# Attention times values with the exponentials standing and 65 value columns passing, division per token, and x turned by the DMA crossbar

## Chip, cores and metric

One core of one Trainium2 chip. The metric is the device time of one execution in microseconds (us), median of several runs. TensorE (PE) has a granted clock that the profile reports beside each stretch; on one core a run cannot be compared with a second die, so a run counts as fast when it lies within 1.5% of the fastest of its kernel.

## The reference

Eight batches of eight heads, 576 tokens, head dimension 64, with a bias that depends on the distance of two tokens and is constant beyond 128; then a feed-forward layer that takes the elementwise maximum of three products.

```python
scores = scale * np.matmul(q, k.transpose(0, 1, 3, 2)) + bias
attn = np.exp(scores - max);  attn = attn / (attn.sum(-1) + 1e-09)
x = (attn @ v).transpose(0, 2, 1, 3).reshape(B * S, H * D)      # 4608 x 512
h = np.maximum(np.maximum(x @ w1, x @ w2), x @ w3)              # d_ff = 768
return h @ w_out                                               # 4608 x 512
```

## The kernel before

Keys lie on the partitions: a score tile holds 128 keys by queries, for two heads (a "head pair") at once. Each head pair of each batch is visited in two halves of 256 queries. The 64 tokens beyond 512 are handled apart: "left keys" (tile `et`) and "left queries" (`scq`). The exponential is multiplied by the exponential of the bias in the band near the diagonal. Attention times values, called the attend, keeps values and a block of 64 ones columns in the array and lets 288 query columns pass. The result comes out with head dimensions on partitions (the form that the FFN wants), and 64 rows of it repeat the row sum.

```python
def attend(b, hp, e4, et, lo, hi, pool=ps_a):       # ps_a: one pair of banks
    ...
    for par in range(2):                             # left keys
        mm(x[par][:, 0:n], lhsT=vt[b % 2][r, hp, :], rhs=et[r, lo:hi], start=True, stop=False)
    for par in range(2):
        for t in range(KT):                          # 4 key tiles, 288 columns each
            mm(x[par][:, 0:n], lhsT=vx[b % 2][:, t, v0 : v0 + P], rhs=e4[:, t, par, lo:hi], ...)
    for par in range(2):                             # reciprocal as exp(-ln(sum)), on ScalarE
        nc.scalar.activation(out=ld[r, 0:n], in_=x[par][d, 0:n], func=ACTF.Ln)
    nc.scalar.activation(out=rd[:, 0:n], in_=ld[:, 0:n], func=ACTF.Exp, scale=-1.0)
    def quotients():                                 # VectorE
        for par in range(2):
            nc.vector.tensor_tensor(out=xT[hp][r, ...], in0=x[par][r, 0:n], in1=rd[r, 0:n], op=ALU.mult)
```

Between the attention instructions the loop puts pieces of the FFN of the batch before. Each product of 512 columns takes one bank of PSUM, the memory that TensorE writes its results to, from a pool of two (`ps_f`); ScalarE copies the first (`m`), VectorE takes the maximum with the second (`m`) and with the third (`hT`), and then the bank is free. The output product goes through `osb` to memory. All stores of `osb` and, from batch 2 on, all q and k transposes are issued by Sync, in program order; before the change the ten transposes for the next batch stand in one block at its first head pair.

```python
    visit(qT, kT, e4, 1)                             # scores and exponentials, second half
    quotients = next_late()                          # emits the attend of a pair before
    times_band(hp, e4, 1, 0, QM)                     # band products on VectorE
    times_band(hp, e4, 2, 0, QM)
    ...
    fill(rate, quotients, lambda: left_queries(qT, kT, e4))     # FFN pieces, quotients among them
```

The softmax here doesn't subtract the row's maximum and nothing guards it: scores larger than these inputs give would overflow.

## Time and profile before

| | before |
|---|---|
| median | 367.65 us (367.58 to 368.91, 3 runs) |
| TensorE, ScalarE, VectorE busy | 335.9, 273.9, 241.8 us |
| batch 1 begins / batch 2's second head pair begins | 45.4 / 94.9 us |
| from there to the end of the span of 367.5 | 272.6 us |
| one half in the middle of the kernel (first, second) | 4.62, 4.57 us |

The starts in the table are those of the first score matmul of a visit in TensorE's timeline. I use 94.9 us as the border of two regions: before it no engine is full, behind it TensorE is. Three of the groups with shapes kept apart (columns: line, engine, operation, result and operand with shapes, count; busy us and mean ns of one; idle time before them and its releaser) belong to the work that the change removes:

```profile
L477 DVE TENSOR_TENSOR xT<-a,rd 64x288 bf16<-64x288 f32 x112 | 50.9, 455 | 28.9 <-ACT rd L472 27.0
L471 ACT ACTIVATE ld<-a 64x288 f32<-64x288 f32 x112 | 45.4, 405 | 10.0 <-PE a L92 7.3
L472 ACT ACTIVATE rd<-ld 128x288 f32<-128x288 f32 x56 | 24.7, 442 | 1.6
```

VectorE waited 27 us for ScalarE's `rd`, but VectorE is not the bound, so this idle time alone costs nothing. What counts is how often TensorE waited for the same chain, and TensorE's waits (total us, times, longest) say: not much.

```profile
PE a L92 <- DVE xT L477: 3.8, 9, 0.9
PE sc L92 <- ACT et L407: 3.4, 5, 0.8
```

### The profile page before, as it was taken

To read this page: it belongs to the slowest core of one execution; us is meant where nothing else is said; L and a number is where in the kernel's file an instruction comes from. 1 tells how busy PE (TensorE), PEld (TensorE's weight loads), DVE (VectorE), ACT (ScalarE), POOL (GpSimd) and SP (SyncE) were. 2 spreads that over 40 slices of the span, in tenths; PEclk is the share of its full clock that TensorE was granted. 3 is DMA by queue.
4 is the path that set the end of the run, shared out by engine and by line. 5 is a ranking of instruction groups with operands and counts; after the bars stand their busy time and mean duration, and the time that the engine had idled before them with its cause. 6 is when DMAs were issued, how large, how long until landed. Compare 5 with 4: busy or idle time off the path is not lost.

```text
span 367.5 us, 6415 instructions
## 1 busy us (share of the span) xinstructions
PE 335.9 (91%) x2364; PEld 185.6 (51%) x2396; DVE 241.8 (66%) x505; ACT 273.9 (75%) x456; POOL 114.4 (31%) x150
## 2 busy tenths in 40 slices
PE   2777888888999999999999999999999999999995
PEld 1444665555455555555555555555555455444442
DVE  6685766555477766776777677777777677545352
ACT  4996897777699988997899889988998798222221
POOL 8736764993850055405550500050000000000000
PEclk9998999988899999999999999999999999999999
DMA  9999999999991099909990992099201100110303
GB/s 163 210 210 160 159 148 144 186 104 142 126 186 12 2 142 150 160 2 119 156 179 3 112 136 75 2 93 142 88 3 57 59 0 2 71 46 0 114 0 117
DMA packets 154600, 36.56 MB, mean 99 GB/s; under 512 B 146624, under 2 KB 149960, under 8 KB 154568
## 3 DMA queue, kind: packets, MB, share of 16 engines
q0 software_dynamic: 109568, 16.59, 65.4%
q1 hardware_dynamic: 43944, 19.29, 25.1%
q8 instruction: 19, 0.31, 0.3%
q10 hardware_dynamic: 1056, 0.26, 0.3%
q14 instruction: 13, 0.11, 0.1%
HBM read 35.39 MB, written 9.45 MB: 122 GB/s over the span
## 4 chain that ended last, share of the span: by engine, by line
PE 72%; ACT 15%; DVE 6%; issue 4%; DMA 1%; another core or an unknown queue 1%; SPq 0%; DVEq 0%; ACTq 0%
PE ps L92 34%; PE a L92 17%; PE pso L92 8%; PE sc L92 8%; ACT e L407 8%; ACT ld L471 3%; PE scq L92 2%; DVE xT L477 2%; DVE osb L313 1%; ACT rd L472 1%; PE sct L92 1%; ACT et L407 1%; DVE hT L300 1%; DMA xT<-in_q_dram 1%
## 5 line engine op out<-in xcount | busy, mean ns | idle before, releaser
L92 PE MATMUL ps<-xT,w_bf 128*128 128x512 bf16 (+1 forms) x695 | 153.2, 360 | 5.2 <-DVE osb L313 2.2
L407 ACT ACTIVATE e<-sc 128x1024 bf16<-128x1024 f32 x128 | 124.1, 1021 | 28.5 <-PE sc L92 28.3
L92 PEld LDWEIGHTS <-w_bf 128*128 128x128 bf16 x720 | 69.1, 99 | 60.5 <-issue 5.0
L401 DVE TENSOR_TENSOR e<-e,band 128x768 bf16<-128x768 bf16 (+4 forms) x140 | 65.2, 477 | 29.5 <-ACT e L407 25.8
L477 DVE TENSOR_TENSOR xT<-a,rd 64x288 bf16<-64x288 f32 (+2 forms) x128 | 58.2, 455 | 32.0 <-ACT rd L472 29.8
L92 PE MATMUL a<-e,vx 128*128 128x288 bf16 (+2 forms) x512 | 76.2, 292 | 0.6 <-DVE e L401 0.6
L92 PEld LDWEIGHTS <-kT 64*128 64x128 bf16 (+1 forms) x740 | 40.8, 97 | 50.5 <-issue 30.5
L92 PEld LDWEIGHTS <-vx 128*128 128x128 bf16 x512 | 45.5, 99 | 29.5 <-issue 18.1
L471 ACT ACTIVATE ld<-a 64x288 f32<-64x288 f32 (+2 forms) x128 | 51.8, 405 | 10.4 <-PE a L92 7.3
L276 ACT ACTIVATE m<-ps 128x512 bf16<-128x512 f32 x54 | 31.7, 587 | 34.0 <-PE ps L92 31.8
L92 PE MATMUL pso<-wo_bf,hT 128*128 128x512 bf16 x209 | 50.7, 380 | 1.3 <-DVE hT L300 0.5
L295 DVE TENSOR_TENSOR m<-ps,m 128x512 bf16<-128x512 f32 x54 | 37.4, 692 | 20.7 <-ACT m L276 15.6
L92 PE MATMUL sc<-qT,kT 64*128 64x256 bf16 x512 | 42.2, 281 | 6.8 <-ACT et L407 3.4
L300 DVE TENSOR_TENSOR hT<-ps,m 128x512 bf16<-128x512 f32 x54 | 37.2, 689 | 15.0 <-PE ps L92 13.7
L155 POOL DMA_DIRECT2D vt<-in_v_dram x16 | 10.2, 655 | 83.6 <-PE a L92 83.6
L147 POOL DMA_DIRECT2D q_sb<-in_q_dram x28 | 25.0, 909 | 31.3 <-DMA qT<-q_sb 27.0
L92 PEld LDWEIGHTS <-hT 128*128 128x128 bf16 x216 | 20.4, 98 | 22.2 <-DVE hT L300 2.1
L472 ACT ACTIVATE rd<-ld 128x288 f32<-128x288 f32 (+2 forms) x64 | 28.3, 441 | 1.7
L147 POOL DMA_DIRECT2D vx<-in_v_dram x32 | 28.5, 928 | 0.2 <-issue 0.2
L147 POOL DMA_DIRECT2D k_sb<-in_k_dram x28 | 24.8, 919 | 11.8 <-DMA w_bf<-in_moe_w_dram 6.8
L313 DVE COPY osb<-pso 128x512 f32<-128x512 f32 x32 | 21.9, 685 | 6.1 <-PE pso L92 5.6
L92 PE MATMUL a<-et,vt 64*128 64x288 bf16 (+2 forms) x128 | 22.3, 286 | 3.8 <-DVE xT L477 3.8
(53 smaller groups left out, 158.8 us busy)
## 6 DMA issues: line engine op xcount, KB each, us to landing
out_dram<-osb SPq DMA_DIRECT2D x36, 256.0 KB, 2.4
vx<-in_v_dram POOLq DMA_DIRECT2D x32, 128.0 KB, 6.0
q_sb<-in_q_dram POOLq DMA_DIRECT2D x28, 128.0 KB, 5.4
k_sb<-in_k_dram POOLq DMA_DIRECT2D x28, 128.0 KB, 5.6
w_bf<-in_moe_w_dram POOLq DMA_DIRECT2D x3, 768.0 KB, 13.5
xT<-in_k_dram SPq DMA_DIRECT2D x6, 128.0 KB, 4.1
wo_bf<-in_moe_w_out_dram POOLq DMA_DIRECT2D x1, 768.0 KB, 7.7
qtail<-in_q_dram POOLq DMA_DIRECT2D x16, 32.0 KB, 5.6
```

What stands on the lines that cost most here:

```text
L92: inorder(nc.tensor.matmul(*args, **kw))
L147: nc.gpsimd.dma_start(out=dst[:, t, h0:h1, :], in_=x[:, t, h0:h1, :])
L155: nc.gpsimd.dma_start(out=diag(dst[b % 2], par, h0, h1), in_=tail_part(src, b, h0, h1, par))
L276: nc.scalar.activation(out=st[fb]["m0"][:], in_=st[fb]["ps0"], func=ACTF.Copy)
L295: nc.vector.tensor_tensor(out=m[:], in0=st[fb]["ps1"], in1=st[fb]["m0"][:], op=ALU.max)
L300: nc.vector.tensor_tensor(out=hT[:, fb * CH : fb * CH + CH], in0=ps2, in1=st[fb]["m"][:], op=ALU.max)
L313: nc.vector.tensor_copy(osb[:], ps[:])
L401: nc.vector.tensor_tensor(out=e4[:, t, :, lo:hi], in0=e4[:, t, :, lo:hi], in1=band[hp][:, :, lo - P * t + P : hi - P * t + P], op=ALU.mult,)
L407: nc.scalar.activation(out=out_, in_=in_, func=ACTF.Exp, scale=inv_sqrt_d)
L471: nc.scalar.activation(out=ld[r, 0:n], in_=x[par][d, 0:n], func=ACTF.Ln)
L472: nc.scalar.activation(out=rd[:, 0:n], in_=ld[:, 0:n], func=ACTF.Exp, scale=-1.0)
L477: nc.vector.tensor_tensor(out=xT[hp][r, b * S + lo : b * S + hi], in0=x[par][r, 0:n], in1=rd[r, 0:n], op=ALU.mult,)
```

## The change

The intent is to swap the operands. The exponentials (128 keys by 128 queries) stand in the array and 65 value columns pass, 64 dimensions and one column of ones. The result then has one token per partition with its sum beside it; the quotient needs one reciprocal per token and head, on VectorE, and the Ln and Exp on ScalarE disappear. In return x is the wrong way round for the FFN, so five crossbar transposes (DMA transfers that transpose on the way, here issued by Sync) per batch turn it (batch 0 is turned on TensorE). The attend's PSUM is now one bank, used in turn with a second. The q and k transposes are spread over three head pairs in place of one block. The diff also puts more FFN pieces into each half of batch 1 (a `rate` of 8 in place of 1) and starts each FFN chunk a half or more later.

```diff
-    ps_a = ctx.enter_context(tc.tile_pool(name="ps_a", bufs=1, ...))      # two tags: one pair of banks
+    ps_a = ctx.enter_context(tc.tile_pool(name="ps_a", bufs=2, ...))      # one tag: two banks in turn
...
-                    x[par][:, 0:n], lhsT=vx[b % 2][:, t, v0 : v0 + P],
-                    rhs=e4[:, t, par, lo:hi], start=False, stop=(t == KT - 1),
...
-            nc.scalar.activation(out=ld[r, 0:n], in_=x[par][d, 0:n], func=ACTF.Ln)
-        nc.scalar.activation(out=rd[:, 0:n], in_=ld[:, 0:n], func=ACTF.Exp, scale=-1.0)
...
+                x[:, 2 * i : 2 * i + 2, :], lhsT=et[:, c], rhs=vl[:, hp, :, 0:AW],          # 130 columns
...
+                        x[:, 2 * i + par, :], lhsT=e4[:, kt, par, c], rhs=v[:, kt, 2 * hp + par, 0:AW],   # 65
...
+            nc.vector.reciprocal(rd[:, 0:n], x[:, 0:n, D])
+            nc.vector.tensor_tensor(out=x_sb[b][...], in0=x[:, 0:4, 0:D]..., in1=rd[:, 0:4]..., op=ALU.mult)
...
+            if b and hp == HP - 1:
+                for t in range(2 * half, 2 * half + 2 + half):
...
+                    inorder(nc.sync.dma_start_transpose(out=xT[:, :, c : c + w], in_=x_sb[b][0:w, t, :]))
...
-                nxt = transposes(b + 1)
...
+        if hp in (1, 2) and b + 1 < B:
+            next(crossbar)                            # two of the ten, five times per batch
```

## The prediction

> **What bounds the kernel now.** I read the page's busy shares first, then the waits of TensorE, then the chain of waits over one batch in the middle, and last the groups of instructions with shapes kept apart. The span is 367.5 us. Busy shares from part 1 of the page:
>
> ```profile
> PE 335.9 (91%) x2364; PEld 185.6 (51%) x2396; DVE 241.8 (66%) x505; ACT 273.9 (75%) x456; POOL 114.4 (31%) x150
> ```
>
> A busy PE proves little, because matmul ends are modelled. The table of 20 us stretches separates two regimes (columns: stretch, PE, PEld, DVE, ACT and POOL busy us with counts, clock, DMA share, GB/s):
>
> ```profile
> 40.00:60.00 20.00, 16.82 (x162) 11.40 (x163) 13.40 (x31) 17.64 (x29) 10.19 (x14) 1.00 1.99 154
> 60.00:80.00 20.00, 16.39 (x157) 11.34 (x155) 12.71 (x28) 15.84 (x27) 19.10 (x25) 1.00 1.84 147
> ...
> 220.00:240.00 20.00, 19.90 (x142) 10.69 (x144) 14.28 (x27) 18.30 (x32) 0.00 (x0) 1.00 0.12 40
> ```
>
> Until about 95 us no engine is full and ACT is the busiest. After that PE is full. The chain of waits in that later region (start, us, what) shows the order of one visit:
>
> ```profile
> 185.13 0.54 PE sc L92 x8
> 185.67 1.21 PE a L92 x10
> 186.88 0.05 issue
> 186.93 1.67 PE ps L92 x7
> 188.61 0.22 PE scq L92 x4
> 188.83 0.87 PE ps L92 x4
> 189.70 0.54 PE sc L92 x8
> ```
>
> Every link is PE: one visit (half a head pair) is 4.57 us, of which the attend "a" is 1.21 us. Once per batch the chain leaves PE (208.1 to 212.5 us: exp, ld, ld, rd, xT, osb), some 0.7 us more than PE work there. A batch repeats every 37.6 us (first score matmuls at 161.2, 198.8 and 236.4 us in the timeline). So the later region pays by PE stream time alone.
>
> The early region is different. In the timeline at 66 to 72 us PE stands 0.67 us for "ACT et", then 0.86 and 0.21 us for "DVE xT". The exponential of the left keys waits behind two Ln, which wait for the attend; the next attend waits until the quotients have freed its single pair of banks.
>
> **What the Trainium skill says.** "TensorE: Matmul & The Clock Gate", section "Back-to-back issue gap", gives N / 2.4 + 2.5 ns warm for an isolated matmul, and about 81 ns per LDWEIGHTS and MATMUL pair at N = 128 as the sustained figure. The same page, "LDWEIGHTS (loading the stationary operand)", gives columns / 1.2, so 107 ns for 128 columns. If either slow figure held, the change would lose. The trace disagrees with both:
>
> ```profile
> 201.35 0.44 PE L92 MATMUL sct<-qT,kT 128*128 128x512 bf16 x3
> 203.77 1.15 PE L92 MATMUL a<-e,vx 128*128 128x288 bf16 x8
> 206.06 0.39 PE L92 MATMUL scq<-qT,kT 128*128 128x128 bf16 x4
> ...
> L92 PE MATMUL sct<-qT,kT 128*128 128x64 bf16 x64 | 7.1, 193 | 0.0
> L92 PEld LDWEIGHTS <-vx 128*128 128x128 bf16 x512 | 45.5, 99 | 29.5 <-issue 18.1 <-DMA q_sb<-in_q_dram 0.4
> ```
>
> The first row is one 512-column and two 64-column matmuls, each with its own 128-column load. It ends 0.44 us after its start; less the last one's 193 ns, the third starts 0.25 us in. The 512 columns take 0.216 (1/2.4 ns each plus 2.5), so the two 64-column ones start about 30 ns apart (28 in the single records). The 288-column ones go at (1.15 - 0.29)/7 = 123 ns, the 128-column ones at (0.39 - 0.22)/3 = 57 ns. A load is shown as 99 ns, but is pipelined ahead and costs the stream nothing. Columns count, not loads.
>
> "VectorE: DVE Perf Modes", section "The TRN2 errata — SBUF-src ops pay a fixed extra latency per instruction", has (N + 151)/0.96 ns for an fp32 tensor_tensor; for 288 elements that is 457, and the quotient rows show 455. I use it for DVE.
>
> "DMA: Bandwidth & Descriptors", section "DMA Transpose (X-bar)", says the plain transpose is issued from Sync or Scalar only and takes 2-byte data. Here all 60 are on SP:
>
> ```profile
> 204.98 5.35 SPq L360 DMA_TRANSPOSE qT<-q_sb  x4
> ```
>
> so about 1.3 us of issue each, and the page's part 6 counts 4 to 5.4 us to landing.
>
> **The change part by part.** *Attend on PE.* Before, one attend is two tail matmuls that run side by side (64-row halves) and eight of 288 columns: 120 + 95 (the load exposed where 64-row tiling ends) + 8 x 123 = 1.20 us. After, the exponentials stand and 65 columns pass: the first half is 2 matmuls of 130 columns (57 ns) and 16 of 65 (65/2.4 + 2 = 29.5 ns), 0.586 us, plus the same 95 ns of exposed load, 0.68 us. The second half adds 5 of 130 columns, 0.97 us. A head pair goes from 2.40 to 1.65 us: 0.75 us saved, although matmuls rise from 20 to 41. The left keys keep their time (512+128 columns for 512+64+64). From 95 us to the end there are 48 of the 64 attends, so 24 x 0.75 = 18 us off PE.
>
> *ACT.* The Ln and Exp of the sums go: 51.8 (ld) + 28.3 (rd) + 3.3 (ones copied into vx) = 83 us, against 64 more columns in 28 exponentials, 28 x 0.05 = 1.5. ACT falls to about 192 us.
>
> *DVE.* Out: 58.2 us of quotients. In, for each head pair: two products of 256 elements from PSUM at 0.42 (the 256-element quotient row has 422 ns), two reciprocals of 4 and 6 columns at about 0.2, two 64-column products at about 0.2, together 1.64, times 32 = 52 us. The left queries' band product costs 0.22 x 32 = 7, less what leaves the last key tile's (640 to 512 elements, 492 to 423 ns). Eight copies of PE-turned batch 0 are about 3 us. DVE stays near 245 us, 73% of a 337 us span, now second. In a steady pair I count 2.5 (bands) + 1.6 + 2.1 (FFN maxima) + 0.7 (osb) = 6.9 us against 8.4 of PE.
>
> *DMA.* 35 transposes join the 60. Per batch that is 5 x 1.3 = 6.5 us of SP, which had long waits for osb. The tokens of one batch are needed only by an FFN chunk that starts about a head pair later (some 9 us against 4 us of issue and 5 of landing). The last chunk's tokens have the previous chunk's 20 us ahead of them, so the tail pays nothing. The q and k transposes are spread over three head pairs instead of one block.
>
> *Early region.* Two banks used in turn replace the single pair, and nothing stands before the left keys' exponential. From 45.4 us (batch 1) to 94.9 the old kernel needs 49.5 us. I sum the new PE work at 36 us: 10 score visits 5.3, attends 8.3, 30 turns of q and k 1.9, left parts 2.5, 256-column FFN 13.1 (24 matmuls are moved in from batch 0), FFN output 4, turning x 0.7. ACT is near 30, DVE near 33. With three engines that near each other I allow 12% of waits: 40.5, so 9 us gained. Before 45.4 us the ACT copies of ones (2.07 us in the chain at 10.7) and six attends' Ln and Exp go, but k of batch 1 is issued until 35 us and lands about 5 later, so I give this stretch 4 us.
>
> *Sum:* 18 + 9 + 4 = 31 us off 367.6, hence 337; I add 1 us for stalls on DVE or crossbar: **338 us**.
>
> **The rivals.** First, short matmuls bound by weight loading or by dispatch. If a pair took 45 ns instead of 29.5, 32 x 32 x 15 = 16 us come back, and the time is about 354; at 60 ns everything is lost. For it: only two short matmuls in a row are ever seen. Against: the load that follows such a matmul is met by the next one 29 ns later too, and 46 instructions fit in one burst between 512-column matmuls.
>
> Second, DVE takes over. If its queue stands behind an exponential, FFN banks (two) are freed late. One extra 1 us per pair is 24 us: about 350 to 360. For it: 82% occupancy in a steady pair. Against: the old kernel ran ACT at up to 18.3 of 20 us in the same stretches without a gap, and the maxima are unchanged.
>
> Third, the crossbar: a landing late by 2 us in each of six batches makes 12 us, about 350. For it: DMA is full until 110 us. Against: after that at least one slice in four of the page's DMA row is nearly empty.
>
> Fourth, the early region gives nothing, because batch 1's loads hold it: 368 - 18 - 3 = 347. Or it gives 15 instead of 13 and the once-per-batch stop disappears (5 more): 331.
>
> **Range and chances.** The 18 us rest on measured spacings; the 13 are a guess between 3 and 17. Eight in ten: 330 to 349. To stay within 2% (above 360.3) nearly all the PE gain must be eaten, so 5%; slower by over 2% needs rates near 60 ns, 2%; faster 93%.
>
> **What would show it.** Right: "a" matmuls of 65 columns about 30 ns apart, an attend of 0.68 and 0.97 us in the chain, a batch of 34.0 to 34.9 us instead of 37.6, ACT near 192 and DVE near 245 us busy, no ld or rd anywhere, PE idle for "DVE xT" gone, batch 2 beginning its second pair near 82 us. Wrong: spacing over 40 ns; PE waiting for "DMA xT" or "DMA kT" by over 3 us in total; DVE busy above 90% in stretches after 100 us with PE below 95%; or batch 1 starting no earlier than 45 us.

## The result, and the profile after

| | before | after |
|---|---|---|
| median | 367.62 us (367.45 to 368.91, 4 runs) | 349.67 us (346.87 to 350.13, 4 runs) |
| span of the profiled run | 367.5 | 348.3 |
| batch 1 begins | 45.4 | 43.1 |
| batch 2's second pair begins | 94.9 | 86.9 |
| from there to the end | 272.6 | 261.4 |
| a half in the middle (first, second) | 4.62, 4.57 | 4.11, 4.69 |

The ratio is 0.9489, 95% interval 0.9434 to 0.9543. Ratios here are the mean time of one kernel's fast runs over that of the other's in the same rounds, so not quite the ratio of the medians. In the two profiled runs 19.2 us were gained: 8.0 before the border and 11.2 behind it.

First the work itself. The page of the changed kernel, and three of its groups with shapes kept apart:

```profile
PE 317.2 (91%) x3052; PEld 179.3 (51%) x3052; DVE 233.8 (67%) x614; ACT 198.3 (57%) x258; POOL 114.8 (33%) x150
```

```profile
L94 PE MATMUL a<-vx,e 128*128 128x65 bf16 x1024 | 46.8, 196 | 1.6 <-DVE e L411 1.3
...
L495 DVE TENSOR_TENSOR x_sb<-a,rd 128x256 bf16<-128x256 f32 x64 | 27.1, 424 | 2.1
...
L493 DVE RECIPROCAL rd<-a 128x6 f32<-128x6 f32 x32 | 6.1, 190 | 1.6 <-PE a L94 1.5
```

ScalarE lost 76 us. The mean of 196 ns of a 65-column matmul is its length from issue to its modelled end, not its cost: in the single records the starts of two that follow one another are 29 ns apart in the median, over runs of eight, and 57 ns where 130 columns pass.

Now the part that did not go as planned. This is the chain of waits in the middle (start, us, what; "e L417" is an exponential, "e L411" a band product):

```profile
143.97 0.86 PE ps L94 x4
144.83 0.34 PE sc L94 x4
...
145.19 1.03 ACT e L417
...
146.25 0.56 DVE e L411
146.81 0.12 DVE rd L493
...
146.95 0.42 DVE x_sb L495
147.37 0.46 DVE e L411
147.84 0.61 DVE hT L305
...
148.49 1.02 PE ps L94 x4
```

Before, this chain was TensorE from end to end, but for one stop per batch. Now it leaves TensorE in the second halves (shown: the fourth head pair of batch 3): an FFN product at 148.49 needs a bank, the bank is freed by the maximum `hT`, and this stands in VectorE's queue behind two band products, the reciprocal and the quotient, which had themselves to wait for the second exponential. All first halves take 4.11 us, and the second ones of third and fourth head pairs 4.69 where my sum of their TensorE work is 4.3 to 4.4. The page's list of waits does not name this one at all, as each is only about 0.3 us; the length of the halves and the chain do. What the list of waits does show, once in the kernel each (the second is in batch 4):

```profile
PE sct L94 <- DMA kT<-ktail: 3.4, 1, 3.4
...
PE ps L94 <- DVE osb L318: 1.5, 1, 1.5
...
PE ps L94 <- DMA xT<-x_sb: 0.9, 1, 0.9
```

The timeline around the first of them (start, us, engine, in brackets the idle time and its releaser):

```profile
73.08 1.29 SPq L366 DMA_TRANSPOSE kT<-ktail  x1
...
74.48 1.04 PE L94 MATMUL ps<-xT,w_bf 128*128 128x256 bf16 x8
...
80.78 0.71 PE L94 MATMUL sct<-qT,kT 128*128 128x512 bf16 x2 [3.39 <-DMA kT<-ktail]
...
81.28 1.91 PE L94 MATMUL ps<-xT,w_bf 128*128 128x256 bf16 x8
```

The table of stretches shows the clock there, third number from the end:

```profile
81.20:83.20 2.00, 2.00 (x12) 1.22 (x12) 0.00 (x0) 0.70 (x1) 1.80 (x3) 0.50 2.21 155
```

The last of batch 2's ten transposes is issued at 73.1, where the old block had issued its last at 60.4. It lands at 80.7, and TensorE stands. And the wait costs more than itself: eight matmuls of the same form take 1.91 us right behind it and 1.04 us before it, as the granted clock is 0.50 for some 3.4 us (about 80.4 to 83.8). "TensorE: Matmul & The Clock Gate" of the Trainium skill, section "What's actually happening", says that the clock halves after an idle window of about 3.4 us. This trace agrees, with 3.39 us of waiting. The two visits of this pair took 11.5 us (75.4 to 86.9).

So there were three suspects for the missing part: banks held behind VectorE's queue in the whole later region; transposes of q and k for batch 2 too late; output stores that wait in Sync's queue behind crossbar transposes.

### The profile page after: what moved, and what is told of

Read it like the earlier page. It is cut to its first block, busy times and chain, and to the rows that moved or that the text cites. A ratio compares the mean times of both kernels' runs of the same rounds, so it can differ in the third digit from the quotient of the medians.

```text
span 348.3 us, 7670 instructions
## 1 busy us (share of the span) xinstructions
PE 317.2 (91%) x3052; PEld 179.3 (51%) x3052; DVE 233.8 (67%) x614; ACT 198.3 (57%) x258; POOL 114.8 (33%) x150
## 4 chain that ended last, share of the span: by engine, by line
PE 55%; DVE 14%; DMA 12%; ACT 9%; POOL 4%; issue 3%; SPq 2%; DVEq 0%; POOLq 0%; ACTq 0%
PE ps L94 30%; PE pso L94 9%; ACT e L417 7%; PE sc L94 6%; PE a L94 6%; DVE e L411 6%; DMA w_bf<-in_moe_w_dram 5%; DVE hT L305 3%; DVE x_sb L495 2%; DMA kT<-ktail 2%; DMA xT<-x_sb 2%; SPq L366 2%; DMA out_dram<-osb 2%; PE sct L94 2%; POOL q_sb L137 1%
## 5 line engine op out<-in xcount | busy, mean ns | idle before, releaser
L94 PE MATMUL ps<-xT,w_bf 128*128 128x512 bf16 (+1 forms) x720 | 158.3, 362 | 4.5 <-DVE osb L318 1.5
L417 ACT ACTIVATE e<-sc 128x1024 bf16<-128x1024 f32 x128 | 124.0, 1021 | 40.8 <-PE sc L94 39.7
L411 DVE TENSOR_TENSOR e<-e,band 128x512 bf16<-128x512 bf16 (+2 forms) x136 | 62.5, 468 | 29.2 <-ACT e L417 28.5
L94 PEld LDWEIGHTS <-kT 64*128 64x128 bf16 (+1 forms) x704 | 37.3, 98 | 47.0 <-issue 25.1
L94 PE MATMUL pso<-wo_bf,hT 128*128 128x512 bf16 x216 | 52.2, 380 | 2.4 <-DVE hT L305 2.4
L300 DVE TENSOR_TENSOR m<-ps,m 128x512 bf16<-128x512 f32 x54 | 37.2, 689 | 17.3 <-ACT m L281 14.8
L94 PE MATMUL a<-vx,e 128*128 128x65 bf16 x1024 | 46.8, 196 | 1.6 <-DVE e L411 1.3
L94 PEld LDWEIGHTS <-e 128*128 128x128 bf16 x1024 | 42.1, 99 | 2.9 <-DVE e L411 2.6
L140 POOL DMA_DIRECT2D q_sb<-in_q_dram x28 | 24.9, 900 | 56.2 <-DMA kT<-k_sb 28.6
L94 PE MATMUL a<-vt,et 128*128 128x130 bf16 x160 | 36.4, 227 | 0.9 <-DVE x_sb L495 0.4
L417 ACT ACTIVATE et<-sct 128x640 bf16<-128x640 f32 (+2 forms) x36 | 23.2, 643 | 12.1 <-PE sct L94 12.0
L495 DVE TENSOR_TENSOR x_sb<-a,rd 128x256 bf16<-128x256 f32 x64 | 27.1, 424 | 2.1
L442 DVE TENSOR_TENSOR et<-et,bandt 128x256 bf16<-128x256 bf16 x32 | 9.3, 291 | 25.2 <-ACT et L417 25.1
```

What stands on the lines that cost most here:

```text
L94: inorder(nc.tensor.matmul(*args, **kw))
L140: nc.gpsimd.dma_start(out=dst[:, t, h0:h1, :], in_=x[:, t, h0:h1, :])
L300: nc.vector.tensor_tensor(out=m[:], in0=st[fb]["ps1"], in1=st[fb]["m0"][:], op=ALU.max)
L411: nc.vector.tensor_tensor(out=e4[:, t, :, lo:hi], in0=e4[:, t, :, lo:hi], in1=band[hp][:, :, lo - P * t + P : hi - P * t + P], op=ALU.mult,)
L417: nc.scalar.activation(out=out_, in_=in_, func=ACTF.Exp, scale=inv_sqrt_d)
L442: nc.vector.tensor_tensor(out=et[:, hi - 256 :], in0=et[:, hi - 256 :], in1=bandt[hp][:], op=ALU.mult)
```

## The experiments

Twelve kernels ran, each beside the kernel before (367.6 to 368.0 us) and all gave correct results, where not said otherwise with three timed rounds. The table splits each profiled run at the border (start of batch 2's second pair, for the kernel before 94.9 us, then 272.6 us to the end). "Gain" is against those two numbers. Forecast for the two gains were 13 and 18, less 1 for stalls.

| run | edit against the changed kernel | median us (range) | ratio, 95% | border us | gain before / behind it |
|---|---|---|---|---|---|
| (after) | | 349.67 (346.87–350.13) | 0.9489, 0.9434–0.9543 | 86.9 | 8.0 / 11.2 |
| again | none | 348.51 (348.10–351.53) | 0.9508, 0.9464–0.9551 | 86.2 | 8.7 / 12.5 |
| ffn3 | three FFN banks, one attend bank | 342.93 (341.55–345.06) | 0.9334, 0.9297–0.9370 | 88.8 | 6.1 / 18.1 |
| band_late | a band product later | 347.39 (347.09–348.28) | 0.9454, 0.9439–0.9469 | 86.9 | 8.0 / 14.2 |
| band_osb6 | that and six osb buffers | 346.23 (343.81–347.44) | 0.9399, 0.9351–0.9446 | 87.2 | 7.7 / 16.0 |
| block1 | batch 2's transposes in one block | 343.22 (341.97–344.22) | 0.9321, 0.9281–0.9362 | 80.9 | 14.0 / 11.9 |
| block | every batch's in one block | 396.94 (395.93–398.17) | 1.0799, 1.0775–1.0824 | 82.0 | 12.9 / −41.8 |
| block_pool | that, stores issued by GpSimd | 345.71 (344.16–346.77, three fast runs) | 0.9383, 0.9357–0.9409 | 80.8 | 14.1 / 8.4 |
| actload | Ln and Exp load put back on ScalarE | 350.70 (349.37–351.69) | 0.9526, 0.9491–0.9561 | 86.2 | 8.7 / 8.9 |
| peturn | x turned on TensorE | 385.16 (384.89–385.25) | 1.0463, 1.0435–1.0492 | 87.7 | 7.2 / −23.0 |
| peturn_ffn3 | that with three FFN banks | 356.59 (355.38–357.27) | 0.9696, 0.9675–0.9718 | 86.7 | 8.2 / 4.9 |
| ffn3_b1_pool | ffn3, block1 and GpSimd stores | 341.27 (339.54–342.55) | 0.9280, 0.9249–0.9312 | 80.1 | 14.8 / 13.1 |
| all4 | that and six osb buffers | 335.38 (334.90–339.01) | 0.9139, 0.9092–0.9187 | 78.6 | 16.3 / 17.6 |

**again.** The changed kernel once more, to have it in the rounds of the others.

> The changed kernel once more, beside the three variants of this call, so that all are read against the same rounds. Every theory expects 347 to 350 us and a ratio to the kernel before of 0.943 to 0.954.

It repeats within 1.2 us. I take 348.5 as the changed kernel's time below, since the first group of experiments shares its rounds.

**ffn3: are the banks the cost?**

```diff
-ps_a bufs=2, ps_f bufs=2
+ps_a bufs=1, ps_f bufs=3
```

> One of the two attend banks is given to the FFN, which then has three (attend one). Theory of the held bank: in the second half of each head pair the last FFN product waits some 0.3 us because the maximum that frees its bank stands on VectorE behind a band product and the quotients; with a third bank nothing waits for that maximum, the half falls from 4.69 to about 4.35 us, and with 22 such halves after 90 us the kernel gets 6 to 8 us faster, about 341 to 343 us. Rival, VectorE is simply too full (some 7 us of work per head pair): a bank more changes nothing in the rate, the half stays at 4.6 to 4.7 us, 347 to 350. Rival, the single attend bank matters (the next attend would wait for the quotients as in the kernel before): slower, 352 or more, with PE waiting for x_sb.

5.6 us faster, and all of it behind the border: 18.1 us gained there, the 18 that were forecast. The timeline of TensorE in one second half, of the changed kernel and then of this one:

```profile
147.97 0.39 PE L94 MATMUL scq<-qT,kT 128*128 128x128 bf16 x4
148.49 1.02 PE L94 MATMUL ps<-xT,w_bf 128*128 128x512 bf16 x4
```

```profile
208.57 0.39 PE L94 MATMUL scq<-qT,kT 128*128 128x128 bf16 x4
208.79 1.03 PE L94 MATMUL ps<-xT,w_bf 128*128 128x512 bf16 x4
```

From the left queries' first matmul to the FFN's first there were 0.52 us, now 0.22, which is the four matmuls' own time. VectorE's part is unchanged; its timeline in this run has the maximum in the same place:

```profile
207.89 0.55 DVE L411 TENSOR_TENSOR e<-e,band 128x768 bf16<-128x768 bf16 x1
208.35 0.68 DVE L305 TENSOR_TENSOR hT<-ps,m 128x512 bf16<-128x512 f32 x1
```

It ends at 209.03, after the product has begun at 208.79: TensorE no longer waits for it. The second halves of third and fourth pairs fall from 4.69 to 4.39 us. Half by half, the 6.9 us between the two runs behind the border are eleven of these at 0.30 us, 0.4 in the last visit, 1.1 in the first second half behind the border, 1.6 at the stop in batch 4 and 0.5 in the other second pairs. The first pairs' second halves stay at 4.67. So the held bank is shown to be the cost, and a third bank also covers the late output copy. The early part got 1.8 us slower, but not by the single attend bank: its waits (3.2 us for `x_sb`) lie at 21 to 28 us, and batch 1 and batch 2 begin at 43.3 and 74.9 us, for 43.1 and 75.4 with two banks. The loss is in batch 2's first pair, where the wait for `kT` is 4.5 us in place of 3.4. So the second attend bank of the change bought nothing that these traces show.

**band_late: the same cost taken away on VectorE's side.** The band product for the third key tile is emitted behind the FFN pieces, so `hT` comes up earlier.

```diff
-        times_band(hp, e4, 2, 0, QM)     # ahead of the FFN pieces of the second half
+        times_band(hp, e4, 2, 0, QM)     # behind them
```

> Only the order on VectorE changes: the second 768-element band product of the second half is placed after the FFN work of that half. The theory of the held bank expects the maximum hT some 0.5 us earlier and the same gain as a third bank: the half at about 4.35 us, 341 to 344 us in all. If VectorE is simply too full (rival), the same work in another order gives no gain: 347 to 350.

Only 1.1 us faster, so the expectation that it would act like the bank was missed. The plain second halves did fall to 4.40 us, which supports the held bank once more. But in each batch's second head pair the second half rose from 4.87 to 5.42 us or more: TensorE waited 3.9 us in all that the list shows for `osb` copies. The time moved rather than went.

**band_osb6: is that for want of output buffers?**

```diff
-osbp bufs=3
+osbp bufs=6
```

> The band product moved late, and six output buffers instead of three. The late band product alone took 0.29 us from each plain second half (4.69 to 4.40) and gave it back where the output tiles stand: PE waited 3.9 us for osb, and osb for its store behind the x transposes on SP. If that is the whole account, six buffers take the osb wait away and the time is 341 to 343.5 us with a second half of 4.40 everywhere. Rival: the lost time moves on to another wait (hT, e) and the time stays at 346 to 348.

The long stop in batch 4 went, but the halves stayed at 5.42 us, with TensorE still waiting 2.7 us, six times, for the copy itself: the copy now stands behind the late band product. Six buffers beside the late band product did not suffice (six buffers alone were not run); reordering one queue moved the wait from `hT` to `osb`.

**block1: are batch 2's transposes too late?** All ten are issued at once at the first head pair of batch 1, as in the kernel before; later batches stay spread.

```diff
+            if b == 1:
+                for _ in transposes(b + 1):      # at hp 0
+                    pass
```

> Only batch 2's q and k transposes are issued in one block at batch 1's first head pair; those of later batches stay spread. The full block made PE stand 46.9 us for osb, because output stores queue on SP behind ten transposes, but removed the wait at 76 us (batch 2's second pair began at 82.0 instead of 86.2 us). If the SP queue and not the DMA load delayed batch 2, this keeps that gain alone: 343 to 345 us, no PE wait for kT over 1 us, no half-clock window at 80 us. If the gain there was given back by what follows, as the rival says: 347 to 349.

5.3 us faster than the repeat. The wait for `kT` is gone, batch 2's first pair takes 6.3 us for 11.5, the border lies at 80.9 us, 6.0 us earlier than in the changed kernel, and the gain behind it (11.9) is within the repeat's spread. This shows that the wait and the half clock behind it cost 5.3 us against the repeat, 6.0 against the first measurement.

**block: why not for every batch?**

> The ten q and k transposes of the next batch are issued in one block at its first head pair again, as in the kernel before, instead of two by two; the x transposes stay. Theory of the SP queue: in batch 1 the spread transposes stand behind output stores that wait for osb, so that the last tail lands at 80.7 us and PE stands 3.4 us and then runs a 3.4 us window at half clock; in one block they land by about 68 us, the wait goes, and 4 to 6 us are gained: 343 to 346. Rival, the loads keep the 16 DMA engines so full until 110 us that the transposes land late wherever they are issued: no gain, 347 to 350, the PE wait for kT still over 2 us.

48 us slower than the changed kernel. The early gain is there (border at 82.0), but in four batches TensorE stands some 12 us. TensorE's waits in this run, and Sync's timeline over one of the four stops:

```profile
PE ps L94 <- DVE osb L318: 46.9, 4, 13.0
```

```profile
111.31 9.04 SPq L513 DMA_TRANSPOSE xT<-x_sb  x5
120.45 1.21 SPq L366 DMA_TRANSPOSE qT<-q_sb  x1
...
132.20 1.26 SPq L366 DMA_TRANSPOSE kT<-ktail  x1
133.56 5.45 SPq L322 DMA_DIRECT2D out_dram<-osb  x4
```

Fifteen transposes follow one another from 111.3 to 133.5 us, and the four output stores behind them in program order come at 133.6. With three `osb` buffers, VectorE cannot copy the next output, the FFN bank stays occupied, and TensorE stops. In the kernel before the block had no x transposes in front of it. The spreading in the change is therefore not a detail; it is what makes the crossbar's turn of x affordable on this queue.

**block_pool: is it the queue or the transfers?** The rival to "stores stand in Sync's order" is that the transposes hold the transfers themselves, whoever issues. The same kernel, the stores (but those of the last chunks) issued by GpSimd:

```diff
-            nc.sync.dma_start(out=out[r0 : r0 + P, :], in_=osb[:])
+            (nc.sync if last else nc.gpsimd).dma_start(out=out[r0 : r0 + P, :], in_=osb[:])
```

> The one-block transposes again (396.9 us, TensorE 46.9 us behind four output copies), but the output stores of all but the last chunks are issued from GpSimd's queue instead of Sync's. If the cause is that stores stand behind fifteen transposes in Sync's own order, the four stops of some 13 us vanish: TensorE waits for DVE osb under 4 us in total and the time is 342 to 350. If the transposes hold the transfers themselves, whichever queue issues them, or if stores on GpSimd stand behind its loads, over 20 us of the waits stay and the time is over 370.

51.2 us came back, and TensorE's wait for `osb` shrank to:

```profile
PE ps L94 <- DVE osb L318: 3.2, 2, 2.1
```

So it was the order of issue. What is left, 3.2 us, may be the transfers' own share or GpSimd's loads ahead of the stores; I did not separate the two.

**actload: does the relief of ScalarE matter?** A rival to "the gain is TensorE's columns" is that the gain comes from ScalarE's 76 us. Two Ln and one Exp of the old size are put behind each reciprocal, with no reader.

```diff
+                nc.scalar.activation(out=ld[r, :], in_=rd[r, 0:1].to_broadcast([64, 288]), func=ACTF.Ln)   # twice
+            nc.scalar.activation(out=l2[:], in_=ld[:], func=ACTF.Exp, scale=-1.0)
```

> ScalarE's relief undone: each attend again has two Ln of 64x288 and one Exp of 128x288 behind its reciprocal, into scratch that nobody reads (the result stays right). ScalarE is back at about 280 us busy. If the gain in the steady part is PE columns alone, the steady halves stay at 4.11 and 4.69 us and only the part before 95 us, where ScalarE was the busiest, gets longer: 350 to 357 us. Rival, ScalarE's relief carried the gain everywhere: halves of 4.5 us and more, 360 or above.

ScalarE is back at 270.5 us busy, and the median rises by only 2.2 us, with ranges that overlap (348.10 to 351.53 and 349.37 to 351.69). But this is a net figure. TensorE now waits for the exponential of the left keys, a line that the changed kernel's list doesn't have:

```profile
PE sc L94 <- ACT et L417: 7.2, 22, 0.8
```

Two stops of the changed kernel absorb most of it. Ahead of the border batch 2 begins at 78.1 us, for 74.1 in the repeat and 75.4 in the first measurement, and the wait for `kT` falls from 3.1 to 0.9 us, so that the border stays at 86.2. Behind it the scores of a plain second half take 0.97 us for 0.59, and the wait for the held bank is gone (0.25 us from the left queries to the FFN product, for 0.52), so that the half takes 4.79 us for 4.69. So in the part ahead of batch 2 ScalarE's relief is worth some 3 to 4 us, and what it is worth in a kernel without the two stops was not tested. As this load has no reader, it tests the occupation of ScalarE and not the old dependence, in which TensorE's next attend waited for the Ln and Exp.

**peturn and peturn_ffn3: what is the crossbar worth?** Here x of every batch is turned on TensorE, as batch 0's is: five transposes per head pair (four of 128 columns, one of 64) through an FFN bank, and copies on VectorE.

```diff
-                    inorder(nc.sync.dma_start_transpose(out=xT[:, :, c : c + w], in_=x_sb[b][0:w, t, :]))
+                turned.append(lambda: x_transposes(hp, half, b))     # emitted among the FFN pieces
```

> The crossbar part of the change undone: x is turned on TensorE for every batch (2 or 3 matmuls of 128 columns each half and a copy from PSUM on VectorE), as the change does for batch 0 alone. The theory that counts PE columns adds 20 x 57 ns = 1.1 us of PE a batch, 8 us in all, and about 20 us of VectorE and one more user of the two FFN banks each half, so 356 to 366 us, with the x wait and the SP delays gone. Rival, the crossbar's queueing on SP is the larger cost: 343 to 350.

At 385.2 us this is slower than the kernel before, and slower than I had expected. Alone it would say that the crossbar is worth 36 us. But the turn takes one of two FFN banks in each half, and a bank held was already shown to stop TensorE. So the same with three FFN banks and one attend bank:

> The version that turns x on TensorE instead of the crossbar (385.2 us), with three FFN banks and one attend bank. Its turn takes an FFN bank in each half. If the two banks are the cost, the third gives most of it back and what stays is the turning work itself, about 0.6 us of columns per head pair over 28 pairs, 17 us: 355 to 366. If the cost is VectorE's extra copy in its queue, which no bank changes, it stays above 376.

356.6 us. The third bank is worth 28.6 us to this version and 5.6 to the changed one; with it on both sides (342.9 for ffn3) the crossbar is worth 13.7 us. In this run all first halves take 4.46 us for 4.11 (three turns, 0.35 us) and the second ones of third and fourth pairs 4.69 for 4.39 (two turns, 0.30), so that a batch takes 36.77 us for 34.67: 2.1 us, six times, 12.6. That fits the 0.6 us a pair that I had expected, but not as columns: starts 55 ns apart would make it below 0.3 us for the five turns. In the first halves the last turn, of 64 columns and 64 rows, starts 152 ns behind the one before it and holds the next product for 132 ns more; in the second halves some 0.29 us pass between the second turn and the next product, where the list names no wait. So the crossbar is worth more than the columns that it saves, and the cause of the rest stays open.

**ffn3_b1_pool and all4: do the gains add?** The two gains act in different regions, so they should.

> Three parts together: three FFN banks and one attend bank, the transposes of batch 2 alone in one block, the output stores on GpSimd's queue. The first two gained 5.6 and 5.3 us alone and act in different stretches (after and before 100 us). If the two causes are separate the gains add: 348.5 - 10.9 = 337.6, and up to 3 us of output stalls go too: 334 to 338. If they draw on the same slack the time stays at 341 to 343. Steady second halves 4.39 us, batch 2's second pair at about 82 us.

341.3 us, so 1.7 us better than ffn3 only; that is outside the expected range and closer to the rival. The border is where it should be (80.1), but 5 us went astray behind it, 4.1 of them in batches 3 and 4. Two lines of this run's timeline, GpSimd's and VectorE's:

```profile
120.25 1.13 POOL L322 DMA_DIRECT2D out_dram<-osb  x2
```

```profile
126.80 0.69 DVE L318 COPY osb<-pso 128x512 f32<-128x512 f32 x1 [3.98 <-DMA out_dram<-osb]
```

The stores were issued by 121.4 us, and the buffer was free only at 126.8: here it is the landing that is slow, while Sync issues its transposes (one at a time from 118.2 to 133.5). With a single attend bank a stop of VectorE soon reaches TensorE: in these two batches it waited 4.0 us for `x_sb` (at 127.9 and 163.7 us), where ffn3 has no such wait. Six `osb` buffers should take that away:

```diff
-osbp bufs=3
+osbp bufs=6
```

> The three parts together (341.3 us) with six output buffers instead of three. There VectorE stood 4.0 us at 122.5 and some 1 us in the next batch because an output copy waited for its buffer, whose store was issued at 121 but had not landed by 126, and TensorE waited 7 us for its attend bank behind it. If it is the number of buffers that turns a late landing into a stop, these 4 to 5 us go: 336 to 338, the third pairs of batches 3 and 4 begin with 4.11 us halves instead of 7.08 and 5.23. If the stores only pile up further, the time stays at 340 to 342.

335.38 us (five rounds), just better than expected, 13.1 us under the changed kernel's repeat (348.51) and 32.6 under the kernel before. Both halves of the third pairs in batches 3 and 4 are back at 4.11 and 4.39 us, a batch takes 34.67 us, and the gains are 16.3 before the border and 17.6 behind it. The page:

```profile
PE 309.7 (93%) x3052; PEld 176.2 (53%) x3052; DVE 234.3 (70%) x614; ACT 198.3 (59%) x258; POOL 130.0 (39%) x178
```

This is the best version.

## Why the prediction was right or wrong

The direction and the mechanism of the gain were right, the size was not: 338 forecast, 349.67 measured, 0.7 us beyond the upper end of the range (348.51 in the repeat). About 30 us were forecast and 19.2 gained in the profiled run. Step by step:

- **Column rate: right.** 29.5 ns per 65 columns and 57 per 130 were forecast, 29 and 57 measured. An attend takes 0.70 and 0.99 us in the chain, for 0.68 and 0.97. The first rival (short matmuls at 45 or 60 ns) is ruled out. The load's own length was no reason for doubt: the trace shows 99 ns, near the 107 that the prediction quotes, and what failed is only that it bounds the spacing. That these 18 us are real is shown by ffn3: 18.1 us behind the border, 34.67 us a batch. In the third and fourth pairs, where both kernels do the same FFN work, it is 0.69 us a pair for the 0.75 forecast; the rest comes from the old stop once per batch.
- **ScalarE: right in size (198.3 for 192 us).** The prediction let it count in the early region alone. That some 3 to 4 us ahead of batch 2 come from it is what actload shows; that it buys nothing later is not shown, as a stop absorbed most of the load there.
- **VectorE: 233.8 us for 245.** The occupation was no danger. The order in its queue was.
- **"I add 1 us for stalls on DVE or crossbar": this is the term that failed.** Behind the border it was 7 us (18 less 11.2; 5.5 in the repeat): 3.3 in eleven second halves of 0.30 us, 1.6 at one stop for an output buffer, the rest in single halves, as the comparison with ffn3 shows. The prediction had the mechanism, as its second rival ("if its queue stands behind an exponential, FFN banks (two) are freed late"), at 1 us per pair; it measured 0.3 us, in two of the four pairs of a batch. I had weighed it by VectorE's share of a pair, and a share does not tell when one instruction of the queue is due.
- **Early region, "40.5, so 9 us gained": too high.** The stretch took 43.8 us (43.1 to 86.9). The third rival, a crossbar landing late, was aimed at x, which cost 0.9 us. It struck q and k of batch 2, once: 3.4 us of waiting and the half clock behind it, 5.3 to 6.0 us by block1. The step "the q and k transposes are spread over three head pairs instead of one block" was written down as free. With it undone for that one batch the early gain is 14.0 us, for the 13 forecast, and the stretch takes 38.4 us. How the 14 divide between ScalarE's relief and the FFN pieces moved into batch 1 is open.
- **Before batch 1, "I give this stretch 4 us": 2.3.** Batch 1 begins at 43.1 and in no run before 42.0. TensorE's list has 1.8 us of waiting for the load of `k_sb`, at 37 to 39 us, which speaks for the fourth rival (the loads hold batch 1); no experiment touched these loads, so it stands untested.
- **Crossbar hidden: partly.** Landing took 3.1 us in the median, less than the 4 to 5.4 used. What the prediction gave no price to is that the stores share Sync's queue; in the changed kernel this cost 1.5 us, in block 46.9.
- **Signs.** One of its signs of being wrong came: TensorE waited 4.8 us in all for `kT` and `xT` (limit 3). Two of its signs of being right did not: a batch takes 35.35 to 36.89 us (forecast 34.0 to 34.9), and batch 2's second pair begins at 86.9 (forecast 82). In all4 these two stand at 34.67 and 78.6.

That all4 ends at 335.4 us, close to the forecast of 338, is partly luck and not a proof of each term, since it has buffers and queues that the changed kernel has not. But its two gains, 16.3 and 17.6, show that the forecast was of a kernel without these stops. Still open are the second halves of 4.67 us in the first head pair of batches 3 to 6, where the output product waits for `hT` (0.3 to 0.5 us each), and the start of batch 1. The 4.78 us in the second pairs hold 14 matmuls of 512 columns where the 4.39 of later pairs hold 12, so no wait is needed to explain them.

## What to carry to other kernels

Count columns for the engine that bounds, and then ask of each buffer of that engine (a PSUM bank first) which instruction frees it and what stands in front of that instruction in its queue; with two buffers in use a queue of 2 us (147.8 + 0.6 less 146.2 in the chain) shows up although the engine is only 67% busy. When a change adds DMA work to an issuing queue, list what else that queue issues, in order: a store behind fifteen transposes stops the bounding engine, and the same store issued elsewhere hardly does. When a load is put back to test an engine's relief, look for a stop that absorbs it before its price is called small. An alternative that loses badly should be run once with its scarce buffer enlarged before it is given up, as turning x on TensorE went from 385 to 357 us by one bank.

## What the Trainium skill lacked or had wrong

- "TensorE: Matmul & The Clock Gate", section "Back-to-back issue gap": it gives about 81 ns per load and matmul pair at N = 128 as the sustained figure, and calls the shorter gap that of an isolated matmul. Here 130-column pairs stand 57 ns apart and 65-column pairs 29 ns, eight in a row, 1024 in all, each with a new 128x128 load. N / 2.4 + 2.5 (56.7 and 29.6 ns) fits both.
- "DMA: Bandwidth & Descriptors", section "Issuing engines are not separate DMA queues": it says that initiating DMAs on several engines "will only save the time on the sequencer it takes to initiate the DMA, which is usually small relative to the DMA itself". With crossbar transposes it is not small: each takes Sync 1.2 to 1.3 us, fifteen kept it for 22 us in block, some waiting included, and moving the stores to GpSimd saved 51.2 us of 396.9. The section's other half, that all run on the same DMA engines, fits ffn3_b1_pool, where a store from GpSimd still landed over 5 us after its issue.
- "VectorE: DVE Perf Modes", section "The three transpose paths": it compares 390 ns on TensorE with 1309 ns for the crossbar for 128x128. The figure of the crossbar is of the order of the issue time here (1.2 to 1.3 us, for a 128x512 source), the landing is 3.1 us in the median, and neither number decides: the crossbar version is 13.7 us faster than TensorE's with three FFN banks, as its time lies beside other work.
- No page that I read tells to follow a PSUM bank to the place of its releaser in another engine's queue; the third bank was worth 5.6 us here, and 28.6 us where x is turned on TensorE.
